# The second head's split operand kept in the pair's tile of halves, with transfers, weight sums and due dates set anew

## The chip, the cores and the metric

The kernel runs on one core of a Trainium2 chip. The metric is the device time of one execution in microseconds (us), as the median of several runs. Beside it there is one profiled execution, in which the hardware recorded when each instruction ran on each engine: TensorE (PE; PEld is its weight load), VectorE (DVE), ScalarE (ACT), GpSimd (POOL) and SyncE (SP), which here only issues transfers.

## The reference

The inputs are q, k and v for 2 batches of 8 heads with 768 tokens of 64 numbers each, 16 centroids for each head, and four weights. The attention keeps a score only where query and key fall to the same centroid. Two layers follow on 1536 tokens of 512 numbers.

```python
q_assign = argmax(q_n @ c_n.T); k_assign = argmax(k_n @ c_n.T)      # by head, normalized
scores = where(q_assign == k_assign, (q @ k.T) / sqrt(64), -1e9)
attn = softmax(scores); x = attn @ v                                # -> [1536, 512]
h = x @ w_in;  g = h * sigmoid(1.702 * h);  x = g @ w_out           # 512 -> 2048 -> 512
h = x @ w2_in; s = h * softmax(h)                                   # 512 -> 1024
y = (s - mean(s)) / sqrt(var(s) + 1e-6) * g_ln @ w2_out             # 1024 -> 512
```

## The kernel before

**Splits.** A product of two fp32 numbers is made of halves: a number is a high half, which the engine multiplies exactly, and a low half, which is the rest. Weights arrive as 64-bit words and are narrowed to 32 bits by three DVE steps (L194, L199, L203), squared and summed on ACT (L216) and by one matmul with ones over the partitions (`tot`, L139, named the *sum* below). From this sum DVE makes a power of two (L145 to L153, and L1243 to L1251 behind it); with it ACT writes the high halves (L237) and DVE the low halves (L240). Nothing that reads a weight's halves can start before its sum.

**Attention.** A pair p (8 of them) is two heads, a unit u (16 of them) is one. The rows of a pair are transposed on PE (L552), ACT copies the high halves (L559, L561) and DVE subtracts to get the low ones (L568); both stand in the tile `hl` of the pair, 128 rows by four planes by 768 tokens: q low, k high, q high, k low. Head i has rows 64i to 64i+63. From `hl` PE makes the logits against the centroids (L582), DVE the argmax, PE turns it (L634), and ACT writes the cluster rows (`oht`, L656).

For the scores of a unit PE needs operands whose rows are in other partitions than those of `hl`, so transfers move them. `OP1` gets the high halves of q and k (place_high, one move of 384 KB for a head), the cluster rows (place_cluster, two moves of 48 KB) and the negated row maxima (`mr`). `OP2` gets both halves, one under the other, for the split products (place_both, two moves of 384 KB for a head). All these moves stand at L659. Two sets of `OP1` and `OP2`, taken in turn by pairs, exist.

A unit has nine tiles of scores of 128 by 512, numbered n = 9u + m. First come the peaks (`sm`, L919), a product of the high halves, from which DVE takes the row maximum (`nma`, L930); the maxima are turned and moved into the operand (`mr`). Then come the scores themselves (`st`, L974 and L975), the exponential on ACT (L983), its cast to fp16 on ACT or DVE (L988), the low half of that (`ph`, L992) on POOL or DVE, and the products with v (`av`, L1007, L1010, L1011). Where a tile *stays*, the exponentials are left in PSUM and DVE makes the low half; otherwise they go to SBUF and POOL can.

**Hidden layer.** Behind the attention come 48 blocks of 12 matmuls (`hps`, L1179), one for each part of w_in and each quarter of the tokens, with gate and halves on ACT (L1186, L1189), DVE (L1197) or POOL. w_in is converted in four groups, the first one in the attention; the conversion of w_out (`wo`) runs beside the blocks, its sum stands among them, and the first projection (L1516) needs its first halves. After that a second plan sets the order of the rest.

**What sets the order.** Every operation of the attention and of the hidden layer is a task in `plan`: costs by engine, a due date, what it comes after, and the PSUM bank that it takes. `order()` goes through time with the planner's own costs; on each engine it picks, of the tasks that are possible first, the one with the smallest due date. The tasks are then written out in the order found, so the order on each engine is fixed in the program, and SP issues its transfers in this order, too: what stands behind a transfer that has to wait waits as well.

## Time and profile before

| | us |
|---|---|
| runs | 597.72, 599.44, 599.91 |
| median | 599.44 |
| profiled execution | 599.53 |
| its span (first to last instruction) | 597.8 |
| first peak matmul starts | 18.69 |
| first hidden block starts | 222.70 |
| sum of w_out runs | 311.51 |
| first projection starts | 321.23 |

The span is 1.7 us shorter than the time of the same execution. Rows of the trace give the start in us from the beginning of the span and a duration in us; in square brackets is the idle time of the engine ahead of it and whom it waited for. Matmuls are pipelined, so their durations overlap, and an engine that is busy all the time need not run at its highest rate. "PEclk" is the share of TensorE's clock that was granted.

### The profile page before, as it was taken

The page shows a single profiled execution, that of the slowest core. Times are in us where ns is not written, and L with a number is a line of the kernel's source. Part 1 is how long each engine was busy: PE and PEld are TensorE (multiplying, and loading weights), DVE is VectorE, ACT ScalarE, POOL GpSimd, SP SyncE. Part 2 cuts the span into 40 slices and gives each one's busy share as a digit, 9 for nine tenths or more (in the row PEclk, how much of TensorE's full clock was granted, in tenths as well). Part 3 has the DMA queues.
Part 4 walks back from the last instruction along what each step waited for, and adds up shares of the span by engine and source line. Part 5 has one row for each costly group of instructions (what it writes and reads, how often), then busy time and mean ns, then how long its engine had stood idle before and what let it go on. Part 6 is the DMA issues. An engine that isn't in the chain of part 4 may idle for free.

```text
span 597.8 us, 12605 instructions
## 1 busy us (share of the span) xinstructions
PE 585.0 (98%) x4784; PEld 386.7 (65%) x4784; DVE 460.3 (77%) x931; ACT 419.2 (70%) x794; POOL 269.2 (45%) x255
## 2 busy tenths in 40 slices
PE   8899999999999999999989999999999999999997
PEld 6687888888888876666645666666655564444444
DVE  6989998799888989888977840884996526997820
ACT  4699989898999988778877446653656623647831
POOL 7269989666787764345653017901200300133100
PEclk9999999999999999999999999999999999999999
DMA  7997979899876127344560440230000430042561
GB/s 189 227 216 163 215 163 184 180 190 185 170 165 119 29 64 203 112 169 135 188 208 1 149 134 2 74 104 0 1 2 0 71 71 0 36 71 72 116 149 53
DMA packets 80884, 68.43 MB, mean 114 GB/s; under 512 B 63748, under 2 KB 66648, under 8 KB 80824
## 3 DMA queue, kind: packets, MB, share of 16 engines
q1 hardware_dynamic: 80824, 67.63, 47.7%
q8 instruction: 37, 0.61, 0.4%
q14 instruction: 23, 0.19, 0.1%
HBM read 34.64 MB, written 3.15 MB: 63 GB/s over the span
## 4 chain that ended last, share of the span: by engine, by line
PE 79%; DVE 11%; DMA 3%; ACT 3%; issue 2%; POOL 1%; SPq 1%; POOLq 0%; DVEq 0%; ACTq 0%
PE bank L1661 20%; PE bank L1482 16%; PE hps L1179 6%; PE bank L1179 5%; PE bank L1516 5%; PE st L974 5%; PE sm L919 5%; PE st L975 4%; PE av L1007 2%; PE av L1011 2%; PE ex L582 2%; PE av L1010 2%; DVE reg L203 2%; DVE reg L199 2%; DVE reg L194 2%
## 5 line engine op out<-in xcount | busy, mean ns | idle before, releaser
L992 POOL TENSOR_TENSOR ph<-p,ph 128x512 f16<-128x512 f32 x108 | 126.9, 1192 | 45.7 <-ACT ph L988 20.4
L1179 PEld LDWEIGHTS <-reg 128*128 128x128 f16 x768 | 75.6, 99 | 49.8 <-issue 1.7
L930 DVE TENSOR_REDUCE nma<-sm 128x1 f32<-128x512 f32 (+1 forms) x144 | 95.9, 680 | 8.8 <-PE sm L919 7.8
L1179 PE MATMUL hps<-xT,reg 128*128 128x384 f16 x576 | 96.2, 330 | 0.0
L1482 PE MATMUL bank<-g,reg 128*128 128x384 f16 x576 | 94.4, 326 | 0.0
L1482 PEld LDWEIGHTS <-reg 128*128 128x128 f16 x576 | 56.4, 98 | 37.2
L1661 PE MATMUL bank<-reg,g 128*128 128x512 f16 (+1 forms) x366 | 75.0, 365 | 0.0
L1194 POOL TENSOR_SCALAR g<-g,scl 128x384 f32<-128x384 f32 x40 | 34.2, 854 | 87.3 <-ACT g L1189 84.3
L1661 PEld LDWEIGHTS <-g 128*128 128x128 f16 x438 | 42.8, 98 | 46.8
L974 PE MATMUL st<-OP 128*128 128x256 f32 (+1 forms) x191 | 70.1, 378 | 2.3 <-DVE nma L930 1.1
L983 ACT ACTIVATE p<-st 128x512 f32<-128x512 f32 x107 | 63.6, 598 | 7.0 <-PE st L975 3.8
L975 PE MATMUL st<-OP 97*128 97x512 f32 (+3 forms) x191 | 62.8, 340 | 0.0
L1007 PE MATMUL av<-vh,ph 128*128 128x65 f16 x576 | 62.2, 194 | 0.0
L1011 PE MATMUL av<-vh,ph 128*128 128x65 f16 x576 | 61.3, 195 | 0.3 <-DVE ph L992 0.2
L1010 PE MATMUL av<-vh,ph 128*128 128x64 f16 x576 | 61.4, 193 | 0.0
L1007 PEld LDWEIGHTS <-ph 128*128 128x128 f16 x576 | 52.8, 99 | 12.5 <-issue 10.3
L919 PE MATMUL sm<-OP 80*128 80x512 f32 x192 | 57.7, 355 | 2.1 <-DMA raw<-in_moe_w_in_dram 0.7
L988 ACT CAST ph<-p 128x512 f16<-128x512 f32 x97 | 58.5, 616 | 1.2 <-PE av L1011 0.6
L1011 PEld LDWEIGHTS <-ph 128*128 128x128 f16 x576 | 53.7, 97 | 0.6 <-DVE ph L992 0.3
L1010 PEld LDWEIGHTS <-ph 128*128 128x128 f16 x576 | 53.8, 97 | 0.1
L1195 POOL TENSOR_TENSOR g<-g,g 128x384 f16<-128x384 f32 x40 | 42.1, 1052 | 3.3
L1864 POOL TENSOR_TENSOR small<-small,mhalf 128x2 f32<-128x2 f32 (+1 forms) x7 | 4.6, 656 | 80.8 <-DVE small L1860 80.8
(252 smaller groups left out, 1168.1 us busy)
## 6 DMA issues: line engine op xcount, KB each, us to landing
OP<-hl SPq DMA_DIRECT2D x48, 384.0 KB, 5.4
raw<-in_moe_w_in_dram SPq DMA_DIRECT2D x24, 512.0 KB, 4.7
raw<-in_moe_w_out_dram SPq DMA_DIRECT2D x24, 512.0 KB, 3.4
xT<-in_v_dram SPq DMA_DIRECT2D x8, 384.0 KB
raw<-in_k_dram SPq DMA_DIRECT2D x12, 192.0 KB, 6.0
raw<-in_q_dram SPq DMA_DIRECT2D x12, 192.0 KB
OP<-oht SPq DMA_DIRECT2D x30, 48.0 KB, 3.7
out_dram<-raw SPq DMA_DIRECT2D x5, 256.0 KB, 2.0
```

The source lines that it names most:

```text
L919: nc.tensor.matmul(t["tile"][:, at], Q1[0:KM, j * P:(j + 1) * P], K1[0:KM, cs], start=True, stop=True)
L930: nc.vector.tensor_reduce(out=out, in_=src, op=ALU.max, axis=AX.X, negate=True)
L974: nc.tensor.matmul(t["tile"][:, at], K2[:, ks], Q2[:, cs], start=True, stop=False)
L975: nc.tensor.matmul(t["tile"][:, at], K1[0:n, ks], Q1[0:n, cs], start=False, stop=True)
L983: nc.scalar.activation(p32s[u, m], t["tile"], AF.Exp, scale=SCALE)
L992: e.tensor_tensor(out=phs[u, m][:, 1], in0=p32s.pop((u, m)), in1=phs[u, m][:, 0], op=ALU.subtract)
L1007: nc.tensor.matmul(av[:, i, :], ph[:, 0, qs], vh[:, u, kt, D:], start=(m == 0 and i == 0), stop=False,)
L1010: nc.tensor.matmul(av[:, i, 0:D], ph[:, 0, qs], vh[:, u, kt, 0:D], start=False, stop=False)
L1011: nc.tensor.matmul(av[:, i, :], ph[:, 1, qs], vh[:, u, kt, D:], start=False, stop=(m == NU - 1 and kt == NJ - 1 and i == NJ - 1),)
L1179: nc.tensor.matmul(self.ps, w1.at(c, m, e), xT[:, x, c, n * TB:(n + 1) * TB], start=(c == 0 and e == x), stop=(c == ND - 1 and e == 1),)
L1482: nc.tensor.matmul(out_, wo.at(f, c, e), lp["g", n][:, x, f, :], start=(f == 0 and e == x), stop=(f == NF - 1 and e == 1),)
L1661: nc.tensor.matmul(out_, data, weight, start=start and i == 0, stop=stop and i == n - 1)
```

## The change

Head 1 has no `OP2` any more. Head 1's halves already stand in rows 64 to 127 of `hl`, in the planes q high and k low; one move puts its other two planes into rows 0 to 63 of these, over head 0's numbers there (`hl<-hl`). So it comes after the logits of the pair and after the two moves that read head 0's rows (`PH` and the first `PB`), and the scores of head 1 read `hl` itself. There are three `hl` tiles instead of two, and the high copies of pair p wait for the last scores of pair p-3 instead of the moves of pair p-2. Each pair has five moves of 384 KB, where it had six.

The planner gets other numbers: costs of transfers, due dates, `LEAD` (how many tiles peaks go ahead), `LAG` (the sum of a weight is planned 3 us behind its squares at the earliest), `ALONE` (tiles with n under 20 no longer stay), and a table `SHIFTS` that moves the due dates of 110 tasks by their numbers. Two of the table's lines are shown.

```diff
--- before.py
+++ after.py
@@ -67,30 +67,30 @@
     CV = 2
     OL = 44
     E1 = -8
-    E2 = 0
+    E2 = -6
     E3 = 0
     NG = 1
     WDUE = 0
-    XDUE = 60
+    XDUE = 30
     VDUE = 15
     VLC = dict(DVE=0.93, POOL=2.55)
-    SOON = 10
+    SOON = 14
     WAHEAD = -80
     WOD = 0
     STAYS = 5
-    ALONE, DRAIN = 0, 120
+    ALONE, DRAIN = 20, 120
     TXM = 1
     XLC = dict(POOL=1.61, DVE=0.93)
     VFIRST = 1
-    VDA = -20
+    VDA = -30
     VDB = 1
-    LDUE = -8
+    LDUE = -14
     RWS = 2
-    URGENT = 0.6
+    URGENT = 0.35
     DEPTH = 1.5
     COLD, WARM = 8.0, 36.0
     CT, WT = 0.2, 0.12
-    ADUE = 5
+    ADUE = 4.5
     AVC = 0.373
     STAY = 1.0
     LOAD = 0.085
@@ -98,7 +98,8 @@
     LN = 512.0
     WLATE = 4
     WAHEAD2 = 6
-    W0, W1 = 20, 100
+    LAG = 3.0
+    W0, W1 = 30, 126
 
     const = ctx.enter_context(tc.tile_pool(name="const", bufs=1))
     wp = ctx.enter_context(tc.tile_pool(name="wp", bufs=1))
@@ -319,12 +320,12 @@
         def __init__(self, buffers, limits, loose=False):
             self.tasks, self.buffers, self.limits, self.loose = [], buffers, limits, loose
 
-        def add(self, cost, due, emit, after=(), take=None, frees=None, kind=None, shared=False):
+        def add(self, cost, due, emit, after=(), take=None, frees=None, kind=None, shared=False, lag=0.0):
 
 
             t = dict(
                 cost=cost, due=due, emit=emit, after=[a for a in after if a is not None], take=take, frees=frees, kind=kind,
-                shared=shared, at=None, id=len(self.tasks), users=[],
+                shared=shared, lag=lag, at=None, id=len(self.tasks), users=[],
             )
             for a in t["after"]:
                 a["users"].append(t)
@@ -347,7 +348,7 @@
 
             def possible(t, eng):
                 near = self.loose and eng == "PE"
-                at = max([free.get(eng, 0.0)] + [a["end" if near and a["eng"] == eng else "ready"] for a in t["after"]])
+                at = max([free.get(eng, 0.0)] + [a["end" if near and a["eng"] == eng else "ready"] + t["lag"] for a in t["after"]])
                 if eng == "SP":
                     at = max(at, dma - DEPTH)
                 if eng == "POOL" or (eng == "DVE" and t["shared"]):
@@ -413,7 +414,7 @@
     rctx = ExitStack()
     actx = ExitStack()
     NP32, NPH = 4, 5
-    NHL = 2
+    NHL = 3
     vh_p = rctx.enter_context(tc.tile_pool(name="vh_p", bufs=1, side="right"))
     p32_p = rctx.enter_context(tc.tile_pool(name="p32_p", bufs=NP32, side="right"))
     ph_p = rctx.enter_context(tc.tile_pool(name="ph_p", bufs=NPH, side="right"))
@@ -427,7 +428,7 @@
     ps_a = actx.enter_context(tc.tile_pool(name="ps_a", bufs=1, space=PSUM))
 
     NU = 9
-    LEAD = 9
+    LEAD = 7
     plan = Plan(
         dict(bank=6, av=2, acc=6),
         dict(st=("bank", 3), sm=("bank", 3), ex=("bank", 4), av=("av", 2), tx=("av", 2), acc=("acc", 6)),
@@ -499,11 +500,12 @@
     NS = 2
 
     OP1 = [[op_p.tile([P, 2, S + 8], F32R, name=f"OP1_{n}_{i}")[:, :, 0:S] for i in range(2)] for n in range(NS)]
-    OP2 = [[op_p.tile([P, 2, S + 8], F32R, name=f"OP2_{n}_{i}")[:, :, 0:S] for i in range(2)] for n in range(NS)]
+    OP2 = [op_p.tile([P, 2, S + 8], F32R, name=f"OP2_{n}")[:, :, 0:S] for n in range(NS)]
 
     def operands(u):
         s, i = u // 2 % NS, u % 2
-        return OP1[s][i][:, 1, :], OP1[s][i][:, 0, :], OP2[s][i][:, 0, :], OP2[s][i][:, 1, :]
+        both = hl[u // 2][:, QH:QH + 2] if i else OP2[s]
+        return OP1[s][i][:, 1, :], OP1[s][i][:, 0, :], both[:, 0, :], both[:, 1, :]
 
     def pad(t):
 
@@ -553,7 +555,7 @@
 
     def turn_high(t, p, e):
         if p not in hl:
-            hl[p] = tok_p.tile([P, 4, S], F32R, tag="hl", name="hl")
+            hl[p] = tok_p.tile([P, 4, S + 8], F32R, tag="hl", name="hl")[:, :, 0:S]
         t = t["tile"]
         if e < 2:
             nc.scalar.copy(hl[p][:, KH + e, 0:512], t)
@@ -667,7 +669,10 @@
         move(OP1[p % NS][i][D:D + C, s, :], oht[p][r:r + C, :])
 
     def place_both(p, i, r, e):
-        move(OP2[p % NS][i][r:r + D], hl[p][i * D:(i + 1) * D, e:e + 2])
+        if i:
+            move(hl[p][0:D, QH:QH + 2], hl[p][D:, e:e + 2])
+        else:
+            move(OP2[p % NS][r:r + D], hl[p][0:D, e:e + 2])
 
     T = {}
 
@@ -685,14 +690,14 @@
         land = {}
         for s in range(2):
             if p == 0:
-                a = add(dict(SP=(0.65, 1.09)), n0 - 8, lambda t, s=s: land.update({s: load_first(s)}))
+                a = add(dict(SP=(0.65, 1.0)), n0 - 8, lambda t, s=s: land.update({s: load_first(s)}))
                 T["L", p, s, 0] = T["L", p, s, 1] = add(
                     dict(DVE=0.5), n0 - 8, lambda t, s=s: arrange(s, land[s]), after=[a], shared=True
                 )
                 continue
             for i in range(2):
                 T["L", p, s, i] = add(
-                    dict(SP=(0.65, 1.09)), n0 + LDUE if p > 1 else -62, lambda t, s=s, i=i: load(p, s, i),
+                    dict(SP=(0.65, 1.0)), n0 + LDUE if p > 1 else -62, lambda t, s=s, i=i: load(p, s, i),
                     after=[at("TT", p - 1, 2)] + late(True) if p > 1 else [],
                 )
         for e in range(3):
@@ -700,8 +705,7 @@
             a = T["TT", p, e] = add(dict(PE=0.43), n0 + 3 * e, lambda t, e=e: turn(t, p, e), after=src, take="ex")
             b = T["TH", p, e] = add(
                 dict(ACT=0.48), n0 + 3 * e, lambda t, e=e, a=a: turn_high(a, p, e),
-                after=[a] + [at("PB", p - NHL, i, n) for i in range(2) for n in range(2)]
-                + [at("PH", p - NHL, i) for i in range(2)],
+                after=[a, at("ST", 2 * (p - NHL) + 1, NU - 1)],
             )
             T["TL", p, e] = add(
                 dict(DVE=0.6 if e < 2 else 0.68), n0 + 3 * e + 4, lambda t, e=e, a=a: turn_low(a, p, e),
@@ -741,18 +745,21 @@
             before = [at("ST", u, NU - 1), at("SM", u, NU - 1)]
             n = n0 + 23 + 4 * i if p else n0 + 10
             T["PH", p, i] = add(
-                dict(SP=(0.65, 1.94)), n, lambda t, i=i: place_high(p, i),
+                dict(SP=(0.65, 2.05)), n, lambda t, i=i: place_high(p, i),
                 after=[T["TH", p, e] for e in range(3)] + before + late(p),
             )
             for s in range(2 if p or i else 0):
                 T["PC", p, i, s] = add(
-                    dict(SP=(0.65, 0.14)), n - 15, lambda t, i=i, s=s: place_cluster(p, i, s),
+                    dict(SP=(0.65, 0.5)), n - 15, lambda t, i=i, s=s: place_cluster(p, i, s),
                     after=[b] + before + ([pads[p, i]] if p < NS else []),
                 )
             for e, r in enumerate((0, D)):
+                if i and not e:
+                    continue
+                out = [T["LG", p, 1], T["PH", p, 0], T["PB", p, 0, 0]] if i else before
                 T["PB", p, i, e] = add(
-                    dict(SP=(0.65, 1.94)), n + 1 if p else -30 + 12 * i, lambda t, i=i, e=e, r=r: place_both(p, i, r, (QH, QL)[e]),
-                    after=[T["TL", p, n] for n in range(3)] + before + late(p or i),
+                    dict(SP=(0.65, 2.05)), n + 1 if p else -30 + 12 * i, lambda t, i=i, e=e, r=r: place_both(p, i, r, (QH, QL)[e]),
+                    after=[T["TL", p, n] for n in range(3)] + out + late(p or i),
                 )
 
 
@@ -799,7 +806,7 @@
         sums = []
         for p in range(NH // 2):
             n = VDA + VDB * p if p else -50
-            a = add(dict(SP=(0.47, 1.09)), n, lambda t, p=p: load_values(p), after=late(p >= VFIRST))
+            a = add(dict(SP=(0.47, 1.2)), n, lambda t, p=p: load_values(p), after=late(p >= VFIRST))
             sums.append(add(dict(ACT=0.82), n + 10, lambda t, p=p: values_bound(p), after=[a]))
 
         def powers(a, n, name):
@@ -879,7 +886,7 @@
         for i in chunks:
             d = due(i)
             prev = add(
-                dict(SP=(0.47, 1.46)), d, lambda t, i=i: w.load(i),
+                dict(SP=(0.47, 1.75 if not after else 1.46)), d, lambda t, i=i: w.load(i),
                 after=[narrows[-n] if len(narrows) >= n else None] + list(scores or late(True)), **kw
             )
             for k, x in enumerate((0.34, 0.6, 0.6) if after else (0.4, 1.0, 0.62)):
@@ -891,7 +898,7 @@
             sums.append(add(dict(ACT=0.61), d + 6, lambda t, i=i: w.square(i), after=[prev], **kw))
         a = add(
             dict(PE=0.1), NH * NU if after else d + 8, lambda t: bound(t, w.squares(c)), after=sums + (after or []),
-            take="acc" if after else "ex", **kw
+            take="acc" if after else "ex", lag=LAG, **kw
         )
         a = add(dict(DVE=0.9), NH * NU if after else d + 8, lambda t, a=a: powers(a), after=[a], frees=a, **kw)
         for i in chunks[0:WLATE if w is wo else w.group]:
@@ -1091,7 +1098,7 @@
             d = n if u else n - SOON
             a = T["ST", u, m] = add(
                 dict(PE=0.47), d, lambda t, m=m: score(t, u, m),
-                after=[T["RW", u, int(m % 3 == 2)] if u < RWS else T["RW", u]] + [T["PB", p, i, e] for e in range(2)], take="st" if u or m >= TXM else "tx",
+                after=[T["RW", u, int(m % 3 == 2)] if u < RWS else T["RW", u]] + [T["PB", p, i, e] for e in range(i, 2)], take="st" if u or m >= TXM else "tx",
             )
             o = a
             a = T["EX", n] = add(
@@ -1292,6 +1299,21 @@
         for u in (2 * p, 2 * p + 1):
             scores_of(u)
     rest_of_layer()
+    SHIFTS = {
...
+        1765: -5, 1777: 6, 1785: -10, 1789: 4, 1806: 4.5, 1813: -5.5,
+    }
+    for i, x in SHIFTS.items():
+        plan.tasks[i]["due"] += x
     order = plan.order()
 
     idle = ps_b.tile([P, 512], F32, tag="av1", name="idle")
```

**DVE around the sum of w_out.** L203 (L204 after) is the last step of the narrowing of w_out, L1197 (L1204) the low half of a hidden block, L145 to L1251 (L146 to L1258) the power from the sum, and L240 (L241) the low halves of w_out. Before:

```order
L199 SCALAR_TENSOR_TENSOR reg_4755<-raw,reg_4755 128x512
L1197 SCALAR_TENSOR_TENSOR g_4756<-hps,scl,g_4756 128x384 x2
L203 SCALAR_TENSOR_TENSOR reg_4755<-raw,reg_4755 128x512
L1197 SCALAR_TENSOR_TENSOR g_4756<-hps,scl,g_4756 128x384
L145 TENSOR_REDUCE scl<-tot 128x1
L147 TENSOR_SCALAR scl<-scl 128x1
```

and further down:

```order
L1248 TENSOR_TENSOR scl<-scl 128x1
L1251 TENSOR_TENSOR scl<-scl 128x1 x4
L240 SCALAR_TENSOR_TENSOR reg_4755<-reg_4755,scl 128x512 x2
L1197 SCALAR_TENSOR_TENSOR g_4756<-hps,scl,g_4756 128x384
L240 SCALAR_TENSOR_TENSOR reg_4755<-reg_4755,scl 128x512 x2
```

After:

```order
L200 SCALAR_TENSOR_TENSOR reg_4747<-raw,reg_4747 128x512
L1204 SCALAR_TENSOR_TENSOR g_4748<-hps,scl,g_4748 128x384
L204 SCALAR_TENSOR_TENSOR reg_4747<-raw,reg_4747 128x512
L1204 SCALAR_TENSOR_TENSOR g_4748<-hps,scl,g_4748 128x384
L146 TENSOR_REDUCE scl<-tot 128x1
L148 TENSOR_SCALAR scl<-scl 128x1
```

and further down:

```order
L1255 TENSOR_TENSOR scl<-scl 128x1
L1258 TENSOR_TENSOR scl<-scl 128x1 x4
L1204 SCALAR_TENSOR_TENSOR g_4748<-hps,scl,g_4748 128x384
L241 SCALAR_TENSOR_TENSOR reg_4747<-reg_4747,scl 128x512 x4
L1204 SCALAR_TENSOR_TENSOR g_4748<-hps,scl,g_4748 128x384
```

One low half of a block has moved from ahead of the last narrowing steps to between the power and the halves of w_out. On PE, where these rows would read alike, the sum stands behind 45 blocks of hidden matmuls and ahead of 3, where it stood behind 44 and ahead of 4.

**SP, the moves of pair 4.** `OP_0_0` and `OP_0_1` are the `OP1` tiles of the two heads of even pairs, the names with 150 and 151 their `OP2`; `OP_1_...` are those of odd pairs. Before:

```order
L1047 DMA_TRANSPOSE xT<-xh 128x6x128
L659 DMA OP_1_0_148<-mr 1x6x128
L1047 DMA_TRANSPOSE xT<-xh 128x6x128
L659 DMA OP_0_0_146<-hl 64x2x768
L659 DMA OP_0_0_150<-hl 64x2x768 x2
L659 DMA OP_0_0_146<-oht 16x768 x2
L659 DMA OP_0_1_147<-oht 16x768 x2
L659 DMA OP_0_1_147<-hl 64x2x768
L659 DMA OP_0_1_151<-hl 64x2x768
L659 DMA OP_1_1_149<-mr 1x6x128
L659 DMA OP_0_1_151<-hl 64x2x768
```

After:

```order
L661 DMA OP_0_0_146<-hl 64x2x768
L661 DMA OP_0_150<-hl 64x2x768 x2
L1054 DMA_TRANSPOSE xT<-xh 128x6x128
L661 DMA OP_1_0_148<-mr 1x6x128
L661 DMA hl<-hl 64x2x768
L661 DMA OP_0_0_146<-oht 16x768 x2
L1054 DMA_TRANSPOSE xT<-xh 128x6x128
L532 DMA raw<-in_k_dram 128x6x64
L661 DMA OP_0_1_147<-oht 16x768 x2
L532 DMA raw<-in_k_dram 128x6x64
L532 DMA raw<-in_q_dram 128x6x64 x2
L661 DMA OP_0_1_147<-hl 64x2x768
```

The three moves into head 1's operands and into `OP2` are fewer by one, the move within `hl` stands behind a row of maxima and ahead of the cluster rows, and the cluster rows of the two heads are parted by a transpose and a load.

**DVE in the second unit.** L930 (L937) is a row maximum, L1022 (L1029) and L1026 (L1033) belong to the output of the unit before, L992 is the low half of exponentials that stayed. Before:

```order
L959 CAST mr<-ex 6x128
L930 TENSOR_REDUCE nma<-sm 128x1
L992 TENSOR_TENSOR ph<-st,ph 128x512
L930 TENSOR_REDUCE nma<-sm 128x1
L1022 TENSOR_SCALAR ri<-av 128x6
L930 TENSOR_REDUCE nma<-sm 128x2
L1024 RECIPROCAL ri<-ri 128x6
L930 TENSOR_REDUCE nma<-sm 128x1
L568 TENSOR_TENSOR hl<-ex,hl 128x512
```

After:

```order
L937 TENSOR_REDUCE nma<-sm 128x2
L966 CAST mr<-ex 6x128
L937 TENSOR_REDUCE nma<-sm 128x1
L1033 TENSOR_SCALAR ri<-ri,scl 128x6
L937 TENSOR_REDUCE nma<-sm 128x1
L1037 TENSOR_TENSOR xs<-av,ri 128x6x64
L937 TENSOR_REDUCE nma<-sm 128x2
L835 TENSOR_REDUCE longest<-ex 8x1
L570 TENSOR_TENSOR hl<-ex,hl 128x512
```

The low half of a tile that stayed is gone from this place; on POOL it stands among the others.

## Rows read from the trace of the kernel before

**Rows 1.** the page, busy time of each engine

```profile
PE 585.0 (98%) x4784; PEld 386.7 (65%) x4784; DVE 460.3 (77%) x931; ACT 419.2 (70%) x794; POOL 269.2 (45%) x255
```

**Rows 2.** windows: length, busy time of each engine (instructions), PE clock, DMA share, GB/s

```profile
18.70:50.00 31.30, 28.48 (x268) 22.06 (x268) 29.19 (x66) 27.78 (x53) 17.68 (x15) 1.00 0.94 223
50.00:222.70 172.70, 170.41 (x2278) 144.50 (x2278) 155.71 (x326) 159.51 (x300) 136.95 (x115) 1.00 0.74 151
222.70:309.40 86.70, 86.70 (x552) 52.47 (x548) 78.93 (x144) 69.49 (x148) 41.57 (x40) 1.00 0.53 163
311.51:315.10 3.59, 3.59 (x13) 1.86 (x14) 1.92 (x11) 2.56 (x5) 2.29 (x4) 0.55 0.42 146
321.20:594.50 273.30, 273.30 (x1534) 149.80 (x1531) 174.70 (x321) 146.08 (x264) 58.45 (x66) 1.00 0.24 59
```

**Rows 3.** waits of PE: line, whom it waited for, us in total, times, longest

```profile
PE tot L139 <- ACT junk L216: 2.0, 1, 2.0
PE st L974 <- DVE nma L930: 1.1, 1, 1.1
PE st L974 <- DVE ph L992: 0.8, 2, 0.6
PE sm L919 <- DMA raw<-in_moe_w_in_dram: 0.7, 1, 0.7
PE sm L919 <- DVE nma L930: 0.6, 2, 0.3
PE sm L919 <- DMA OP<-oht: 0.5, 1, 0.5
PE st L974 <- ACT p L983: 0.4, 1, 0.4
```

**Rows 4.** timeline of PE around L139: start, us, instructions merged, idle before

```profile
297.76 11.70 PE L1179 MATMUL hps<-xT,reg 128*128 128x384 f16 x71
311.51 0.40 PE L139 MATMUL tot<-wss,ones 128*128 128x16 f32 x2 [2.04 <-ACT junk L216]
311.75 9.64 PE L1179 MATMUL hps<-xT,reg 128*128 128x384 f16 x48
```

**Rows 5.** timeline of DVE around L139

```profile
309.97 0.67 DVE L203 SCALAR_TENSOR_TENSOR reg<-raw,reg 128x512 uint32<-128x512 uint32 x1
313.05 0.62 DVE L1197 SCALAR_TENSOR_TENSOR g<-hps,scl,g 128x384 f16<-128x384 f32 x1 [2.41 <-ACT g L1189]
313.58 0.17 DVE L145 TENSOR_REDUCE scl<-tot 128x1 f32<-128x16 f32 x1
...
317.20 1.41 DVE L240 SCALAR_TENSOR_TENSOR reg<-reg,scl 128x512 f16<-128x512 f32 x2 [0.58 <-ACT reg L237]
```

**Rows 6.** timeline of ACT ahead of L139

```profile
310.73 0.63 ACT L216 ACTIVATE junk<-reg 128x512 bf16<-128x512 f32 x1 [0.90 <-DVE reg L203]
```

**Rows 7.** the page, DMA issues: instructions, KB each, median us to landing

```profile
OP<-hl SPq DMA_DIRECT2D x48, 384.0 KB, 5.4
```

**Rows 8.** DMA issues from 36 to 110 us, the same columns

```profile
OP<-hl SPq DMA_DIRECT2D x23, 384.0 KB, 7.4
```

**Rows 9.** timeline of the DMA queue of SP, pair 4

```profile
97.95 1.95 SPq L1047 DMA_TRANSPOSE xT<-xh  x1
99.99 2.97 SPq L659 DMA_DIRECT2D OP<-hl  x3
103.86 5.20 SPq L659 DMA_DIRECT2D OP<-oht  x4
```

**Rows 10.** timeline of all engines, row of maxima of unit 2 and its first scores

```profile
54.13 0.83 SPq L659 DMA_DIRECT2D OP<-mr  x1
...
57.44 0.40 PE L974 MATMUL st<-OP 128*128 128x512 f32 x1
```

**Rows 11.** groups by line, the low half of the exponentials

```profile
L992 POOL TENSOR_TENSOR ph<-p,ph 128x512 f16<-128x512 f32 x108 | 126.9, 1192 | 45.7 <-ACT ph L988 20.4 <-DVE ph L988 8.9 <-PE sm L919 4.8
...
L992 DVE TENSOR_TENSOR ph<-st,ph 128x512 f16<-128x512 f32 x36 | 24.6, 682 | 2.6 <-ACT ph L988 2.4
```

10 rows, old and new, of the table SHIFTS are left out of this document.

## The prediction

> **What bounds the kernel now.** The page's first line is read first: TensorE (PE) is busy 98% of the span [rows 1]. That does not say that it works at its peak, so the windows come next, stage by stage [rows 2]. From 222.70 to 309.40 us and from 321.20 to 594.50 us PE is busy for every microsecond at the full granted clock: matmuls stand back to back, and nothing that another engine does there can be felt. What can move lies in three other places. From 18.70 to 50.00 us, the first two heads, PE works 28.48 of 31.30 us and VectorE (DVE) 29.19. From 50.00 to 222.70 us, the rest of the attention, PE lacks 2.29 of 172.70 us. The third place is around 311 us.
>
> The waits of PE say for whom [rows 3]. The longest one behind the start is 2.0 us at L139, the matmul that sums the squares of w_out, on ScalarE's (ACT) square L216. The others lie in the attention: DVE's row maximum holds up scores (1.1) and later peaks (0.6), the low half of the exponentials on DVE (L992) holds up scores (0.8), and two peak matmuls wait for data, 0.5 on the cluster rows and 0.7 on a weight load (that matmul does not read a weight, so I take the cluster rows moved beside it for the true cause). With the 0.4 at L983 and three of 0.2 that are not shown these make 4.7 us. On TensorE's timeline the wait at L139 shows a second cost [rows 4]: ahead of it 71 hidden-layer matmuls take 11.70 us, 0.165 us each; the 48 behind it take 9.64 us, 0.201 each, where 7.91 were to be had. The granted clock explains it: 0.55 from 311.51 to 315.10 us [rows 2], near the lower of the two levels (1.2 GHz beside 2.4), after PE had stood idle for two microseconds. So this one wait costs 2.04 + 1.73 = 3.77 us.
>
> Here a page of the Trainium skill bears on the reading: Perfetto Trace Analysis, section Identifying the Most-Contended Engine, says that the busy share of matmuls is no good measure of how near a kernel is to its peak. The trace agrees: both stretches around L139 read as fully busy, and by busy time alone the wait would be worth 2.04 us, by the rate 3.77.
>
> **The wo sum.** It now stands one block of 12 matmuls later: the order has 45 blocks ahead of it and 3 behind (44 and 4 before), with the same work on DVE and ACT ahead. PE reached it at 311.51 - 2.04 = 309.47 us; one block more is 12 x 0.165 = 1.98, so 311.45. The last narrowing on DVE began at 309.97 [rows 5], the last square on ACT at 310.73 [rows 6], and the sum ran at 311.51: nearly met, 0.06 us stays. If DVE or ACT are later than before, up to the whole 2.04 comes back, with the low clock. Behind the sum the cover shrinks from 48 matmuls to 36, 36 x 0.165 = 5.94 us. Under it lie the powers, then the first high half on ACT and the first low half on DVE, which the first projection reads. From the rows on DVE: the sum ended at 311.91; the first step of the powers began at 313.58, behind an L1197 that ran from 313.05; the first low half began at 317.20 and, as one of two in 1.41 us, ended near 317.9. From the sum's start that is 6.4 us; without the wait of 1.14 us for ACT ahead of that L1197 it is 5.3. Against 5.94 the stall lies between 0 and 0.5 us; I take 0.2, since the wait of 1.14 belongs to a PE that had stopped. Term: -3.77 + 0.06 + 0.2 = **-3.5 us**, between -3.8 and 0.
>
> **Operand of the second head.** Head 1's split operand no longer is a tile of its own: half of it is already in its rows of the pair's tile, and one move (hl<-hl) fills the other half. That takes one of six moves of 384 KB from each pair (48 of them now, 40 then); each lands 5.4 us after its issue in the median of all, and 7.4 from 36 to 110 us, where transfers are thickest [rows 7, 8]. The transfers themselves are mostly hidden: PE waits 1.2 us on them in all. But SP issues in order, and in pair 4 three such moves hold it for 2.97 us and the cluster rows' four for 5.20 more [rows 9]; the peak matmul that needs them waits the 0.5 us. One move less, and the cluster rows of head 0 no longer queued with those of head 1, frees about 1 us (2.97 / 3) and 2.60 (5.20 / 2); each of the two waits is smaller. Term: **-1.2 us**, between 0 and -1.2.
>
> What it costs: hl<-hl overwrites rows that two other moves read, so SP stops at it until these have landed. In the order it stands behind the row of maxima (OP<-mr) and ahead of the cluster rows in pairs 4 to 7. Between the second of the two moves and it stand a third move (1.0), a transpose (1.95) and the mr row (0.83) [rows 9, 10], 3.8 us that are needed anyway; in pairs 5 and 7 no transpose is among them, which leaves 1.8. With 5.4 us to landing SP then holds 1.6 or 3.6, and the move's own issue adds 1.0: 2.6 us, less than the 1 + 2.6 that the cluster rows gain, or 4.6, which is 1.0 too much. Mr stands ahead of it, and is needed late: in the tightest case before, unit 2, mr is issued at 54.13 us and its first scores start at 57.44 [rows 10]. LEAD falls from 9 to 7, which brings mr nearer to its scores in most units. Pair 0's hl<-hl stands behind all v loads and could hold up unit 1's scores. For pairs 5 and 7 that is 2 x 1.0 us; half of it I take to be covered: of the four pairs' peaks only two wait for data now [rows 3]. I add **+1.0 us** for new waits, between 0 and the rival below. Three hl tiles for two take the wait of ACT's high copies for moves away; it stood on no path of PE.
>
> **Work off DVE.** With ALONE at 20 the tiles n = 1, 6, 11 and 16 no longer stay in PSUM: their low half goes from DVE (0.68 us) to GpSimd (1.19 us) [rows 11]. One cast more stands on DVE. That is 3 x 0.68 = 2.0 us less on DVE where it is busy 29.19 of 31.30 us and where its waits cost 1.1 + 0.6 + 0.8 = 2.5. I take half of that as recovered: **-1.2 us**, between 0 and -2.5. GpSimd has 17.68 of 31.30 us filled there; 4.8 more fit.
>
> **The rest.** The listed due dates, the planner's new transfer costs and the loads of k and q ahead of the centroids at the start move rows among themselves; the work on PE is the same. I cost them at nothing, since what they change is hidden by a busy PE wherever the windows are full; at the start, where nothing hides it, from -1 us (one issue, 2.97 / 3) to +2.
>
> Sum: 599.53 (the profiled execution: span 597.8 and 1.7 around it) - 3.5 - 1.2 + 1.0 - 1.2 = 594.6. The median of the runs is 599.44, 0.1 lower; 594.6 stands for both.
>
> **Rivals.**
> *More comes free.* All visible waits of the attention go and no new one appears: 599.53 - 3.77 - 4.7 = 591.1 us; a start 1 us earlier gives 590. For it: DVE and SP are both relieved. Against it: only DVE's share is really lessened, and some 110 listed tasks have new neighbours. Chance 0.14.
> *It does nothing that lasts.* The sum meets its square late again, since ACT or DVE carry more ahead of it, or the stall only moves behind the sum: 1 us of wait and a low clock, 2 of the 3.5 lost, and the transfers were hidden anyway: 597 to 601 us. For it: the margin at the sum is 0.06 us. Against it: the full rate of PE on both sides. Chance 0.20.
> *SP is held by hl<-hl, and it gets slower.* It decides as soon as SP's hold, landing time less what was issued in between and with its own 1.0, exceeds the 3.6 us that the cluster rows gain. With 7.4 us to landing it is 7.4 - 3.8 + 1.0 = 4.6 in pairs 4 and 6, 1.0 too much, and 6.6 in pairs 5 and 7, 3.0 too much: 8.0 us. With the 1.2 us at the cluster rows not gained, and in place of the 1.0 already counted, this gives 594.6 + 8.0 + 1.2 - 1.0 = 602.8. The Trainium skill's page DMA: Bandwidth & Descriptors, section Two DMAs through the same engine are not ordered, has the issuing engine wait for the first transfer's completion before it issues one that depends on it; by that rule all of the remaining time to landing is held, and no run so far shows how long that is. For it: the wait is new, in a queue that all transfers share. Against it: PE waited for transfers only 1.2 us in all. Chance 0.14.
>
> **How the numbers follow.** My forecast, all terms about as worked out (592.5 to 596.4 us), has a chance of 0.52. A measurement of this kernel tells about 0.5%, 3 us, from no change: faster is below 596.4. So faster 0.52 + 0.14 = 0.66, same 0.20, slower 0.14. Time: 594.6 us. The range goes from the far end of the first rival, 590, to 600, which takes in most of the second and leaves out the third.
>
> **What would show it.** In the profile after: no wait at the last sum, or one under 0.3 us, and the granted clock at 1.00 through to the first projection, whose matmuls follow at once; from the last sum to the first projection some 6.3 us instead of 9.9; peaks that wait on no cluster rows; the first hidden block about 1.5 us earlier than 222.70. Wrong would be: new waits of scores on hl<-hl or mr in several pairs, SP held for microseconds by its own moves, or a sum that waits as before.

## The result: 0.9% faster, and the profile after

The changed kernel takes 594.87 us in the median (593.02 to 596.73) where the kernel before, beside it on the same chip, takes 600.12. The ratio is 0.9911 with a 95% interval of 0.9890 to 0.9932: 4.1 to 6.6 us less. The profiled execution takes 594.86 us, 4.67 less than that of before. 594.6 was forecast.

The timeline of TensorE (PE) cuts the 4.7 us of span into stages. Start, duration, instructions merged, idle time before:

```profile
19.27 0.94 PE L926 MATMUL sm<-OP 80*128 80x512 f32 x2
...
221.66 2.11 PE L1186 MATMUL hps<-xT,reg 128*128 128x384 f16 x12
...
310.56 0.29 PE L140 MATMUL tot<-wss,ones 128*128 128x16 f32 x2
310.70 6.01 PE L1186 MATMUL hps<-xT,reg 128*128 128x384 f16 x36
316.55 18.69 PE L1538 MATMUL bank<-g,reg 128*128 128x384 f16 x114
```

The first peak is 0.6 us later than before (18.69), the first hidden block 1.04 earlier (222.70). From there to the first projection 94.89 us pass, where it was 98.53: 3.64 us. Behind it the two kernels agree to 0.01 us (278.31 and 278.30 to the end of the execution). The sum of w_out, which waited 2.04 us [rows 4], waits for nothing, and the 36 matmuls behind it take 0.167 us each; from the sum to the first projection 5.99 us pass, 9.72 before (the prediction's 9.9 runs to the end of the last block). The clock stays up, as a window shows (length; busy time of PE, PEld, DVE, ACT, POOL; clock, DMA share, GB/s):

```profile
306.00:320.00 14.00, 14.00 (x90) 8.55 (x88) 8.47 (x28) 11.80 (x23) 6.39 (x9) 1.00 0.22 76
```

The longest waits of PE, besides one of 2.3 us at the start that both kernels have; in the attention they stand at other places than in [rows 3]:

```profile
PE st L981 <- ACT p L990: 1.2, 1, 1.2
PE sm L926 <- ACT oht L658: 0.7, 1, 0.7
PE ex L474 <- DVE chl L466: 0.5, 1, 0.5
```

And the windows of the first two heads, of the rest of the attention, and of one stretch in the first part, in the same columns:

```profile
18.70:50.00 31.30, 28.49 (x241) 22.18 (x242) 26.74 (x59) 24.15 (x47) 15.08 (x14) 0.95 0.81 192
50.00:221.66 171.66, 171.18 (x2307) 145.60 (x2307) 157.16 (x327) 160.05 (x305) 143.22 (x119) 1.00 0.67 137
36.00:42.00 6.00, 4.79 (x26) 3.81 (x23) 3.03 (x9) 5.02 (x10) 3.88 (x4) 0.72 0.61 122
```

Against [rows 2], PE lacks 0.48 us in the rest of the attention, not 2.29. In the first two heads it lacks as much as before, 2.81 us (2.82), and now at a granted clock of 0.95: whatever DVE and SP gave there was lost again to something else. The timeline of ScalarE (ACT) shows what:

```profile
33.77 0.88 ACT L658 ACTIVATE oht<-ex,apart 64x768 fp32r<-64x768 bf16 x1
34.56 0.84 ACT L779 ACTIVATE vh<-xT 128x768 f16<-128x768 f32 x1
35.30 0.18 ACT L779 ACTIVATION_READ_ACCUMULATOR vh<-xT 128x1 f32 x1
36.24 0.86 ACT L779 ACTIVATE vh<-xT 128x768 f16<-128x768 f32 x1 [0.76 <-DMA xT<-in_v_dram]
37.00 0.18 ACT L779 ACTIVATION_READ_ACCUMULATOR vh<-xT 128x1 f32 x1
37.09 1.06 ACT L990 ACTIVATE p<-st 128x512 f32<-128x512 f32 x2
```

The squares of v (L779), whose due dates VDA moved from -20 to -30, stand ahead of the cluster rows (L658) and of the exponentials (L990); the last of them waits for v's own transfer, and PE waits for the exponentials behind it, 1.21 us up to 37.72. From 38 to 40 us the granted clock is 0.50.

### The profile page after: what moved, and what is told of

Its sections match the earlier page's. It is cut to its first block, busy times and chain, and to the rows that moved or that the text cites. A ratio compares the mean times of both kernels' runs of the same rounds, so it can differ in the third digit from the quotient of the medians.

```text
span 593.1 us, 12562 instructions
## 1 busy us (share of the span) xinstructions
PE 583.3 (98%) x4783; PEld 387.7 (65%) x4783; DVE 455.5 (77%) x929; ACT 415.6 (70%) x792; POOL 277.4 (47%) x259
## 4 chain that ended last, share of the span: by engine, by line
PE 85%; DVE 8%; ACT 3%; DMA 2%; issue 1%; SPq 1%; POOL 0%; ACTq 0%; POOLq 0%; DVEq 0%
PE bank L1683 20%; PE bank L1504 16%; PE hps L1186 8%; PE st L981 6%; PE sm L926 6%; PE bank L1186 5%; PE bank L1538 5%; PE st L982 5%; PE av L1014 3%; PE av L1018 3%; PE av L1017 3%; PE ex L584 2%; PE ex L554 1%; DMA xT<-in_v_dram 1%; DVE reg L200 1%; DVE reg L204 1%
## 5 line engine op out<-in xcount | busy, mean ns | idle before, releaser
L999 POOL TENSOR_TENSOR ph<-p,ph 128x512 f16<-128x512 f32 x112 | 133.1, 1208 | 41.1 <-ACT ph L995 24.4
L937 DVE TENSOR_REDUCE nma<-sm 128x1 f32<-128x512 f32 (+1 forms) x144 | 95.9, 680 | 7.4 <-PE sm L926 6.5
L1186 PE MATMUL hps<-xT,reg 128*128 128x384 f16 x576 | 94.6, 326 | 0.2 <-DVE g L1204 0.2
L1201 POOL TENSOR_SCALAR g<-g,scl 128x384 f32<-128x384 f32 x40 | 37.4, 936 | 80.9 <-ACT g L1196 80.7
L990 ACT ACTIVATE p<-st 128x512 f32<-128x512 f32 x111 | 64.5, 599 | 6.3 <-PE st L982 4.8
L982 PE MATMUL st<-OP 97*128 97x256 f32 (+3 forms) x191 | 62.8, 341 | 0.0
L926 PE MATMUL sm<-OP 80*128 80x512 f32 (+1 forms) x192 | 56.8, 359 | 1.2 <-ACT oht L658 0.7
L926 PEld LDWEIGHTS sm<-OP 80*128 80x128 f32 x192 | 33.9, 192 | 8.0 <-DVE nma L937 2.3
```

The lines of the kernel that those rows point to most:

```text
L926: nc.tensor.matmul(t["tile"][:, at], Q1[0:KM, j * P:(j + 1) * P], K1[0:KM, cs], start=True, stop=True)
L937: nc.vector.tensor_reduce(out=out, in_=src, op=ALU.max, axis=AX.X, negate=True)
L982: nc.tensor.matmul(t["tile"][:, at], K1[0:n, ks], Q1[0:n, cs], start=False, stop=True)
L990: nc.scalar.activation(p32s[u, m], t["tile"], AF.Exp, scale=SCALE)
L999: e.tensor_tensor(out=phs[u, m][:, 1], in0=p32s.pop((u, m)), in1=phs[u, m][:, 0], op=ALU.subtract)
L1186: nc.tensor.matmul(self.ps, w1.at(c, m, e), xT[:, x, c, n * TB:(n + 1) * TB], start=(c == 0 and e == x), stop=(c == ND - 1 and e == 1),)
```

## The experiments

Each kernel was timed beside the kernel before on the same chip, though not all kernels on one chip; ratios are to the kernel before, and the changed kernel's own is 0.9911. 0.001 is 0.6 us. In the code, three dots stand for lines left out.

**The sum of w_out, moved by one block.** `behind(task, mark)` takes a task, and what in between depends on it, out of the finished order and puts it behind another; in this kernel the order on all other engines stays. First in the kernel before:

```diff
...
+    total = T["SUM", wo, 0]
+    behind(total, <the next hidden block in the order>)
```

> The kernel before, with the sum of w_out written one hidden block of 12 matmuls later; every other row on every engine stands as before. If the wait at the sum and the low clock behind it are the 3.77 us that the rows give, and 0.06 us of waiting and 0.2 us behind the sum stay: 3.5 us less than before, ratio 0.994, PE idle under 0.3 us at the sum, granted clock 1.00 behind it. Rival: the stall only moves behind the sum, since 36 matmuls do not cover the power and the first halves: less than 1.5 us gained.

Measured: ratio 1.0002 (0.9986 to 1.0019), so nothing was gained, as the rival had it. The timeline of PE, and one row of DVE's:

```profile
314.06 0.29 PE L139 MATMUL tot<-wss,ones 128*128 128x16 f32 x2
314.20 6.01 PE L1180 MATMUL hps<-xT,reg 128*128 128x384 f16 x36
320.04 1.16 PE L1530 MATMUL bank<-g,reg 128*128 128x384 f16 x6
321.91 0.65 PE L1530 MATMUL bank<-g,reg 128*128 128x384 f16 x3 [0.70 <-DVE g L1198]
322.95 1.30 PE L1530 MATMUL bank<-g,reg 128*128 128x384 f16 x7 [0.39 <-ACT g L1187]
```

```profile
321.24 0.62 DVE L1198 SCALAR_TENSOR_TENSOR g<-hps,scl,g 128x384 f16<-128x384 f32 x1 [0.25 <-ACT g L1190]
```

There is no wait at the sum, but two in the projection, for the halves of the last hidden blocks, which stand behind the power and the halves of w_out on DVE and ACT. So part of the stall did move. But only part: in this one execution the stretch from the first hidden block (225.50) to the first projection is 94.54 us, 4.0 shorter than before, and the two waits behind it make 1.1 us; the time is the same because its attention is 2.8 us longer, at a granted clock of 0.50 from 32 to 36 us. Over all runs nothing remains of the gain, and why is open. Then the other way round in the changed kernel, the sum ahead of the block:

> The changed kernel, with the sum of w_out one hidden block earlier, behind 44 blocks as in the kernel before; every other row stands as in the changed kernel. If the block is what takes the wait away (the prediction's step): the wait of 2 us and the low clock come back, 3.5 us more than the changed kernel. Rival, from the changed kernel's trace, where the last square of w_out ends at 308.4 us and PE would reach the earlier sum at 308.6: the conversion itself comes earlier, no wait, within 0.3 us of the changed kernel.

Measured: 0.9935 (0.9913 to 0.9956):

```profile
309.37 0.29 PE L140 MATMUL tot<-wss,ones 128*128 128x16 f32 x2
309.51 7.96 PE L1187 MATMUL hps<-xT,reg 128*128 128x384 f16 x48
```

From the first hidden block (222.38) to the first projection (317.30) it takes 94.92 us, as in the changed kernel, and there is no wait. So the block is not what took the wait away.

**The tail as before, the attention as changed.** The tail is the hidden layer with the conversion of its weights; LAG and the shifts are taken from its tasks.

```diff
+    tail_0 = min(t["id"] for t in plan.tasks if t["tail"] == 2)
+    for t in plan.tasks[tail_0:]:
+        t["lag"], t["due"] = 0.0, t["due"] - SHIFTS.get(t["id"], 0)
```

> The changed kernel, with the hidden layer and the conversion of w_in's later groups and of w_out planned as in the kernel before (no LAG there, no shifts of those tasks); the attention's order is that of the changed kernel. If the new tail is worth what the profiled executions show between the first hidden block and the first projection (98.5 us before, 94.9 after): 3.6 us more than the changed kernel, 1.8 of it only in executions where the clock falls behind the wait. Rival, after the sum moved by one block alone gained nothing: the tail as planned here has no wait either, and the gain hangs on when the attention ends; within 0.7 us.

Measured: 0.9971 (0.9949 to 0.9993), 0.0060 or 3.6 us above the changed kernel. The wait and the low clock are back, in the waits, the timeline and a window; the first row of the last fence is the last square of w_out in the changed kernel, the second the same one here, where the first hidden block starts at 222.11:

```profile
PE tot L140 <- ACT junk L217: 2.4, 2, 2.1
```

```profile
312.06 0.56 PE L140 MATMUL tot<-wss,ones 128*128 128x16 f32 x2 [2.05 <-ACT junk L217]
312.46 9.47 PE L1186 MATMUL hps<-xT,reg 128*128 128x384 f16 x48
```

```profile
312.00:316.00 4.00, 3.94 (x15) 2.15 (x16) 2.27 (x11) 2.62 (x6) 2.64 (x4) 0.57 0.35 131
```

```profile
307.65 0.63 ACT L217 ACTIVATE junk<-reg 128x512 bf16<-128x512 f32 x1 [0.23 <-DVE reg L204]
311.28 0.63 ACT L217 ACTIVATE junk<-reg 128x512 bf16<-128x512 f32 x1 [0.90 <-DVE reg L204]
```

**LAG alone, in the tail of the kernel before.**

```diff
...
-            take="acc" if after else "ex", **kw
+            take="acc" if after else "ex", lag=3.0 if after else 0.0, **kw
```

> The kernel before, with the 3 us of LAG on the weights' sums in the hidden layer and nothing else; the attention's order is that of before. If LAG makes the tail's gain: 2 us less in executions at the full clock, up to 3.6 less where the clock falls behind the wait, no wait at the sum and none at the first projection. Rival, as with the sum moved one block by hand: the square comes no earlier, and the stall moves behind the sum; 0 to 1 us less.

Measured: 0.9976 (0.9959 to 0.9993), 1.4 us less than before, between what the two expectations name. The trace has no wait at the sum, 24 matmuls behind it, and 0.3 us at the projection:

```profile
310.51 0.63 ACT L216 ACTIVATE junk<-reg 128x512 bf16<-128x512 f32 x1
319.20 0.49 PE L1516 MATMUL bank<-g,reg 128*128 128x384 f16 x2
```

Counted from its first hidden block (224.69), the last square ends at 86.45 us and the first projection starts at 94.51: in the trace LAG alone brings the conversion forward and gives nearly all of the 3.64 us. That the runs gain only 1.4 is not explained; this execution's attention was 2.0 us longer than that of before, with a granted clock of 0.72 from 30 to 36 us.

**The squares of v later.** On ACT the last four squares stand behind the cluster rows and the exponentials that they held up; `act` lists the four ACT operations that followed the last square:

```diff
...
+    for p, m in ((4, 1), (5, 1), (6, 3), (7, 3)):
+        behind(T["VB", p], act[m])
```

> The changed kernel, with the last four squares of v on ScalarE moved behind the cluster rows and three exponentials that stand after them; no other engine's order changes. If these squares, which wait for v's transfers, hold up the exponentials and with them PE (0.7 and 1.2 us, and a granted clock of 0.81 and 0.62 from 36 to 42 us): 1.5 to 3 us less than the changed kernel, about 592.5 us, and the clock at 1.00 there. Rival: PE then waits for the move within the pair's tile or for the next pair's halves, which are as late: within 0.5 us of the changed kernel.

Measured: 0.9899 (0.9881 to 0.9918), median 593.06 us, all six runs between 592.57 and 593.42; profiled execution 592.87, 1.99 less than the changed kernel's. This is the fastest kernel of the study. The same window as above, and the waits of PE:

```profile
36.00:42.00 6.00, 5.02 (x46) 4.03 (x46) 4.74 (x17) 5.89 (x14) 3.80 (x5) 1.00 0.70 144
```

```profile
PE ex L140 <- ACT p L991: 1.0, 1, 1.0
PE sm L927 <- DVE nma L938: 0.6, 3, 0.2
```

Both waits are gone and the clock is full; one of 1.0 us has come at PE's sum over the squares, which now comes too early. The intervals of the two ratios overlap, so only the profiled executions and the narrow spread speak for a gain over the changed kernel. The spread also says where it lies: at a granted clock of 1.000 the changed kernel took 593.02 and 593.16 us, this one 592.57 to 593.32. What differs is that four of the changed kernel's six runs are at 0.997 or 0.994, and none here is below 0.999. Moving that sum back by four operations:

> The changed kernel with the four squares of v moved as before, and PE's sum over these squares four operations later, since in the kernel with the squares moved PE waits 1.0 us at that sum. If the wait is the sum's own: 1 us less than with the squares moved alone, about 592 us. Rival: the scores behind it wait for the next exponentials instead; within 0.4 us of it.

Measured: 0.9909 (0.9884 to 0.9934), 594.54 us, 0.6 us above the kernel with the squares alone by the ratios and 1.5 by the medians, on two chips. The microsecond did not come: the sum's wait goes, 0.8 us come at a transpose, for a copy on ACT (L591). The rival was right that another wait takes its place, though not which one, and the 0.4 us that it allowed were exceeded.

**The four low halves back on DVE.**

```diff
+    for n in (1, 6, 11, 16):
+        T["RE", n]["eng"] = "DVE"
```

> The changed kernel, with the four low halves of n = 1, 6, 11 and 16 back on VectorE (from SBUF, not from PSUM) at their places in the order; nothing else changes. If they are worth what the prediction took (half of what DVE's waits cost): about 1.2 us more than the changed kernel. Rival: the first two units of the changed kernel are held by ScalarE and transfers, and VectorE is busy 26.74 of 31.30 us there: within 0.5 us.

Measured: 0.9967 (0.9944 to 0.9991), 0.0056 or 3.4 us above the changed kernel. The window behind the first two heads, first of the changed kernel, then of this one:

```profile
50.00:60.00 10.00, 9.84 (x121) 7.89 (x120) 9.96 (x23) 9.93 (x18) 9.92 (x10) 1.00 0.69 132
```

```profile
50.00:60.00 10.00, 8.51 (x90) 6.56 (x88) 9.97 (x21) 9.21 (x15) 9.06 (x9) 1.00 0.72 141
```

DVE is full in both; the four low halves, 0.68 us each, run on it at 30.12, 38.73, 48.35 and 58.37 us, and PE comes 1.3 us short in these 10. Behind it the granted clock falls (0.60 from 60 to 62, 0.55 from 62 to 64 us). At 1.000 this kernel took 594.95 and 595.59 us, some 2.2 more than the changed kernel; as far as two runs of each can tell, the rest of the 3.4 goes with the clock.

**The move within the pair's tile, twice.**

```diff
-            move(hl[p][0:D, QH:QH + 2], hl[p][D:, e:e + 2])
+            for _ in range(2):
+                move(hl[p][0:D, QH:QH + 2], hl[p][D:, e:e + 2])
```

> The changed kernel, with every move within the pair's tile issued twice, the same rows to the same place, so that there are again 48 moves of 384 KB; no other order changes. If a move less for each pair is worth what the prediction took, about 1.2 us more than the changed kernel, with a wait of peaks for the cluster rows; SP is held 0.6 to 1 us more for each pair. Rival: the transfers were hidden anyway, and what the attention gained came from the order: within 0.4 us of the changed kernel.

Measured: 1.0284 (1.0248 to 1.0321), 22 us above the changed kernel, far outside what I expected of it. The second move writes what the first one writes, so SP waits at it for the first one's landing. The waits of SP's queue, and those of PE:

```profile
SPq L661 <- DMA hl<-hl: 33.0, 8, 7.9
```

```profile
PE sm L927 <- DMA OP<-oht: 4.5, 3, 2.1
PE ex L554 <- DMA raw<-in_k_dram: 3.0, 2, 2.8
PE ex L554 <- DMA raw<-in_q_dram: 2.6, 1, 2.6
```

So it measures above all the price of what the third rival feared, 4.1 us of hold in each pair; the second move's own bytes and issue are in the 22 us too, and a granted clock of 0.94 from 60 to 222 us. In the changed kernel itself the move is not held in any of the eight pairs. SP's queue in pair 4:

```profile
104.07 0.78 SPq L661 DMA_DIRECT2D OP<-mr  x1
104.96 0.64 SPq L661 DMA_DIRECT2D hl<-hl  x1
105.69 1.94 SPq L661 DMA_DIRECT2D OP<-oht  x2
```

**Bytes and issues put back.** Two more moves for each pair, into rows of the operand that no product reads, first of 26 rows each (156 KB; the expectations' 160 is rounded), then of one row (6 KB). They stand ahead of the move within the tile, so they put that off as well:

```diff
+            for x in range(2):
+                move(OP1F[p % NS][x][102:P], hl[p][D:D + 26, e:e + 2])
```

> The changed kernel with two more moves of 160 KB for each pair, from the pair's tile to rows of the first operand's tile that no product reads, issued just ahead of the move within the pair's tile; nothing waits for them. They put back more than 0.8 of the bytes of the move that the change dropped, and two issues of 0.65 us. If bytes and SP's time limit the attention: 1 us or more above the changed kernel, with peaks waiting for cluster rows. If, as the doubled move suggests, it is only a wait for a landing at the head of SP's queue that hurts: within 0.7 us of the changed kernel.

> As the kernel with two more moves for each pair, but each move carries one row of 6 KB instead of 26 rows of 160 KB: the same issues on SP at the same places, with hardly any bytes. The two moves with their bytes cost 2.8 to 3.9 us against the changed kernel at equal granted clock. If that is SP's time to issue (16 more issues of 0.65 us): the same here, 596 us or more at the full clock. If it is the bytes in the transfer engines: within 0.7 us of the changed kernel, 593 us at the full clock.

Measured: with 156 KB each 0.9991 (0.9967 to 1.0015), 4.8 us above the changed kernel; with 6 KB each 0.9934 (0.9914 to 0.9955), 1.4 above it, and not clear of it. The intervals of the two stand apart, so the bytes cost something beyond the issues. Neither expectation fits alone. In neither trace does SP wait for a landing of these moves. The first expectation also had peaks waiting for cluster rows. With the bytes none does, but a transpose waits 0.9 us for them and two waits of 1.3 are for casts on ACT; with the issues alone one peak waits for them, 1.0 us.

**Operand without the numbers, numbers without the table.** The first has all planner numbers of before, the second all of the change but an empty `SHIFTS`.

> The changed kernel with all planner numbers of the kernel before (LAG 0 and an empty table of shifts among them): the operand of the second head and the three tiles alone, planned anew. If the operand carries the attention's gain (2.2 us and more between 55 and 221 us) and the sum keeps its wait: about 598 us. If the numbers carry it: 600 us or more, with waits for transfers as before.

> The changed kernel with an empty table of shifts; all other numbers and the operand stay. If the table of 110 shifted due dates is what makes the gain in the attention: 2 to 4 us more than the changed kernel, waits of peaks and scores back in the trace, the sum of w_out still without a wait (LAG stays). Rival: the operand and the few named numbers carry it: within 1 us.

Measured: 1.0030 (1.0007 to 1.0052) and 0.9992 (0.9970 to 1.0014). The operand alone is slower than before; with the numbers it is level; the table carries the rest, 0.0081 or 4.9 us. In the second trace PE waits again, for loads of k (1.5), a copy on ACT (1.0) and, in the hidden layer, for halves of w_in (0.9 and 0.8); from its first hidden block (222.53) to the first projection (320.40) it takes 97.87 us, 3.0 more than in the changed kernel. In the traces this is most of the 3.8 us by which the two spans differ.

The first trace has what the prediction charged for the move within the tile. The waits of SP's queue and PE's longest, and SP's queue in pair 4, where the move within the tile stands right behind two moves of halves:

```profile
SPq L661 <- DMA OP<-hl: 6.1, 4, 1.9
PE st L981 <- DVE ph L999: 2.4, 2, 1.5
```

```profile
102.41 1.99 SPq L661 DMA_DIRECT2D OP<-hl  x2
106.36 0.59 SPq L661 DMA_DIRECT2D hl<-hl  x1
```

Four times SP is held ahead of its issue, in pairs 0, 1, 4 and 5, for 6.1 us in all. Without the table it is 2.5 us, also in four pairs, and in the changed kernel nothing. PE's own waits in the first trace are nearly all for DVE, so what the hold costs there is not shown.

## Why the prediction was right

The time came out, and the largest term with its size; the mechanism behind that term did not, nor did the +1.0, nor what was costed at nothing. That the sum lands within 0.3 us of the measured time is therefore partly luck.

*The wo sum, -3.5 us.* The size was right: 3.64 in the profiled executions, 3.6 by undoing the tail. Of the 3.77, 1.73 is the low clock, which not every execution has. The step that failed is "with the same work on DVE and ACT ahead". Counted from the first hidden block, the last square of w_out ended at 88.66 us before, ends at 86.62 now, and at 89.80 with the tail undone (for the first, 310.73 + 0.63 - 222.70). I read the later place of the sum as the cause, and it was a companion: had the conversion not come earlier, a stall of 1.1 us would have stood behind the sum, as the kernel with the sum moved by hand shows, where I had taken 0.2 and at most 0.5. My list of what lies under the 36 matmuls left out the low halves of the last hidden blocks, which queue on DVE behind the power. LAG alone brings the square to 86.45 us; in the runs it gives a part of the gain, 1.4 us. With the new attention the table is needed as well: without it the square ends at 88.89.

*The second head's operand, -1.2 and +1.0 us.* The waits for moved cluster rows went, as forecast; the 0.7 us at a peak now are put down to ACT's writing of such rows. The +1.0 did not come: SP reaches the move when what it depends on has landed. The mechanism is real, though. Under the old numbers SP was held 6.1 us in four pairs; the planner's new numbers, which I costed at nothing, took the hold away, and the moves of halves now land 4.0 us after their issue, where I reckoned with 5.4. With the move doubled, 33.0 us of hold cost 22 us. By the rival's formula it would be 12: in each of eight pairs 4.1 us of hold and 1.0 for the issue, less the 3.6 gained. Of the rest, the second move's bytes and issues are some 5, an estimate from the moves put back; what makes the remainder is open. That a move less is worth having is borne out by the moves put back, 1.4 us for the issues and 4.8 with bytes, more than the 1.2 I took; by itself, under the old numbers, it gained nothing and lost 1.8 us.

*Work off DVE, -1.2 us.* The direction was right, and 3.4 us for the way back, 2.2 at the full clock, is more than the 1.2 that I took; that kernel reads its operands from SBUF, so it does not undo the change exactly.

*The rest, at nothing.* This failed in both directions. The squares of v cost the waits of 0.7 and 1.2 us and the clock, about 2 us of the profiled execution, and the first peak came 0.58 us later; for the start I had kept -1 to +2. Where the clock stays up, moving the squares gains hardly anything, so their price is mostly the clock's. And the table of shifts, which I did not cost, is what turns operand and numbers into a gain. The terms that were too small and those left out offset each other, which no step of mine foresaw: the attention gave 1.04 us in the trace, where my three terms made 1.4.

## What to carry to other kernels

A wait that is taken away by moving its waiter has to be looked for again behind the new place: list every instruction that shares the queues under the new cover, also those of other work that the next stage reads. A due date brought forward for an instruction that waits for a transfer costs whatever stands behind it on its engine, so a load and the first instruction that reads it should not be moved together. And where a scheduler's order is fitted to one program, undo parts in the finished order rather than plan anew: the operand planned anew came out 1.8 us slower than before, more than the 1.2 us that its move was taken to gain.

## What the runs showed of the hardware that I had not expected

Executions of one program differ in how much of TensorE's clock they are granted, and in the median the time follows. Of 45 executions of the kernel before on one chip, 14 had a mean granted clock of 1.000 and a median of 597.7 us, 8 had 0.997 and 599.5, 18 had 0.994 and 600.5. The clock is not all: one of the 14 took 600.23 us. In most of the traces such a difference is one or two stretches of a few microseconds near the lower level (1.2 GHz), in the first two heads or behind the sum of w_out, after PE has waited: 2.04 us ahead of the 0.55 before, 1.21 ahead of the 0.50 now. The changed kernel's runs fall in the same classes: 593.02 and 593.16 us at 1.000, 594.86 to 595.04 at 0.997, 596.73 at 0.994. With the squares of v later all six were at 0.999 or 1.000. Why the same program falls in some executions and not in others stays open; so a wait of 1 or 2 us has to be costed twice, as idle time and as a chance of the clock behind it.
